# A gated linear attention with an MLP on one core: another order table for all engines, and 64 fill-in matmuls of 512 columns for 134 of 256

## The chip, the core and the metric

The kernel runs on one core of a Trainium2 chip. The core has five engines that run side by side, each in the order of its own instruction queue: PE (TensorE, matmuls), ACT (ScalarE), DVE (VectorE), POOL (GpSimd) and SP (SyncE, which here only issues DMAs). The metric is the time of one execution on the device in microseconds, as the median of several runs.

## The reference: what is computed

For each of 4 batches and 8 heads, over 768 steps, a state of 48 x 48 complex numbers decays by a gate per row and takes up the outer product of k and v; y is q times the real part of the state. Then y, with the heads put side by side (384 columns), goes through a layer norm and an MLP (384 to 1536 to 384, ReLU) and is added to its result.

```
scale = min(mag, 0.999) / (mag + 1e-6);  a = (a_re + i a_im) * scale
for t: S = a[t][:, None] * S + k[t] v[t]^T
       y[t] = q[t] . Re(S)
x = y, heads side by side;  out = x + relu(layernorm(x) * g @ w_ch1) @ w_ch2
```

## The kernel before, in words

The 768 steps of each batch are cut into 6 chunks of 128, and two chunks make a pair: 12 pairs, P = 0 to 11, and 24 chunks, n = 2P and 2P + 1. For a pair, `pair_ops` (line 393) adds named operations. The gates become a running log-decay: ln, iv, r, r2, u on ACT, DVE and POOL, then l and lc on DVE, and dec, a matmul with triangular ones on PE; e and en on ACT are the exponentials of its sum. The angles go th (arctan) on ACT, ph on PE (a running sum, taken over from pair to pair by car), sin and cos on ACT; in the first three pairs the cosine is made by a second sum, qt. The logarithms and the sines need different tables on ACT, and the operations tab.log and tab.trig load them. From this come ke = k * en, qe = q * e, and the products ks and qs with sin and cos. These are transposed to ksT and qsT, either on PE (kT, qT, then a copy out of PSUM) or by a DMA issued from SP (line 599). Then am = ksT' qsT and its masked copy atm, the state G from gm, and y and its copy x. After bn (the norm's sums), xtr and xT (the transpose of x), the MLP follows: mm1 (line 722), relu (lines 739 and 741), mm2 (line 754). The scale of the norm, rstd, is applied at the end in ot, on DVE at once or as oa on ACT and ot on POOL, and st stores it (line 777). The first weight of the MLP is corrected once by wp on PE and wc on DVE, so that the norm's mean needs no step of its own.

No program orders the work while it is built: the order is the table `PLAN` (lines 39 to 144), a list of 1160 entries such as `relu.0.0:A0`. An entry names an operation, the engine (P for PE, A for ACT, V for DVE, G for POOL, S for SP) and, where it uses PSUM, the bank. `Graph.run` (line 164) emits the operations in this order, so each engine's queue is the order of its own letters in the table. An entry with `@name` is made to wait for another operation besides its operands (line 208): such waits put POOL and DVE in turns.

A DMA is issued by the engine that the table names: SP's queue or ACT's (`ring`, line 285). Loads of k, q and vf (line 404) are one chunk of 192 KB each, are and aim (line 445) 384 KB for a pair, in halves for pair 0. Buffers go in rings (`RINGS`): three for are, aim, q and k, two for vf, five for ot. An issue on ACT's queue has its place among ACT's arithmetic. w1b and w2b, the weights, are loaded from POOL (wl).

In the table before, ACT issues aim.0.0 and aim.0.1, 18 of the 24 vf loads (from vf.3 on) and 19 of the 25 stores; SP issues the rest and the 25 transposing DMAs.

The fill-ins `warm.0` to `warm.133` (line 787) are matmuls on constants, with a result that nobody reads. They stand in PE's queue between its first real operations, up to am, y and ph of the first two pairs.

Of the kernel before, what the change touches and what calls it, by code (L numbers as in the profile page):

```python
# [59 lines left out]
warm.123:P0 car.0.1:A4 wgc:V cos.0.0:A1 qt.0.1:P4 ph.1.0:P6 k.1.1:S ks.0.1.1:V cos.0.1:A4 qs.0.1.1:V th.2.0:A  # L60
qs.0.0.1:V qs.0.1.0:V wp.1:P5 ks.0.1.0:V sin.1.0:A6 qs.0.0.0:V ks.0.0.0:V qT.1:P4 wc.1.2:V5 tab.log.2:A qT.0:P1
qsT.1:V4 kT.1:P0 qs.1.0.1:G@wc.1.2 dec.2.0:P2 car.1.0:V6 ln.3.0:A warm.124:P4 qsT.0:V1 warm.125:P4 wp.0:P4 e.2.0:A2
are.4.0:S wc.1.0:V5 kT.0:P1 en.2.0:A2 vf.1.0:S ksT.1:V0 ksT.0:A1 wc.0.0:V4 vf.1.1:S am.1:P2 warm.126:P0 wc.1.1:V5
iv.3.0:A warm.127:P0 am.0:P0 wc.0.2:V4 qt.1.0:P6 tab.trig.3:A warm.128:P5 warm.129:P5 warm.130:P5 warm.131:P5
wc.0.1:V4 warm.132:P5 warm.133:P5 atm.0:V0 ph.2.0:P4 r.3.0:G@wc.0.1 cos.1.0:A6 k.2.0:S v.0:A wp.2:P6 atm.1:V2
aim.4.0:S sin.2.0:A4 gm.0:P7 ke.1.0.0:G y.0:P0 G.0:V7 k.2.1:S x.0:A0 qt.2.0:P4 ke.1.0.1:V gm.1:P7 cos.2.0:A4 y.1:P1
q.2.0:S qs.1.0.0:V xtr.0:P0 ks.1.0.0:V x.1:A1 qT.2:P3 th.3.0:A ks.1.0.1:V qT.3:P5 qsT.2:V3 xtr.1:P1 q.2.1:S xT.0:A0
r2.3.0:G@ks.1.0.1 kT.3:P4 qsT.3:A5 xT.1:V1 kT.2:P2 ksT.3:V4 mm1.0.0.0:P0 G.1:V7 q.3.1:S tab.log.4:A v.1:G am.3:P4
ksT.2:V2 mm1.0.0.1:P0 are.5.0:S ke.2.0.0:G atm.3:V4 ln.4.0:A mm1.0.1.0:P2 q.3.0:S wl.3:G mm1.0.1.1:P2 relu.0.0:A0
wc.2.0:V6 am.2:P4 wc.2.2:V6 relu.0.1:A2 gm.2:P7 k.3.0:S atm.2:V4 ph.3.0:P0 qe.2.0.0:G@wc.2.2 G.2:A7 k.3.1:S iv.4.0:A  # L70
y.3:P2 wl.4:G wc.2.1:V6 y.2:P3 x.3:A2 gm.3:P7 pad.ks.2:G u.3.0:A mm1.0.2.0:P4 x.2:V3 r.4.0:G@wc.2.1 bn.3:V xtr.2:P6
xtr.3:P3 mm1.0.2.1:P4 xT.2:A6 xT.3:V3 G.3:V7 tab.trig.5:A mm1.1.1.0:P2 relu.0.2:V4 qe.2.0.1:G are.6.0:S mm1.1.1.1:P2
sin.3.0:A0 wl.5:G mm1.1.2.1:P6 bn.0:V vf.2.0:S relu.1.1:A2 mm1.1.0.1:P4 pad.qs.2:G l.3.0:V mm1.1.2.0:P6 abs.3.0:A0
r2.4.0:V mm1.1.0.0:P4 th.4.0:A car.3.0:V0 mm2.0.0:P2 relu.1.0:A4 ke.2.0.1:V mm2.1.0:P3 qs.2.0.1:V vf.2.1:S cos.3.0:A
lc.3.0:V mm2.2.0:P4 qs.2.0.0:V bn.2:V tab.log.6:A qT.4:P5 mm2.1.1:P3 bn.1:V rstd.1:G dec.3.0:P0 ks.2.0.1:V u.4.0:A
ks.2.0.0:V mm2.0.1:P2 rstd.0:G en.3.0:A0 l.4.0:V ksT.5:S mm2.2.1:P4 e.3.0:A0 lc.4.0:V ln.5.0:A relu.1.2:V6
qe.3.0.1:G@lc.4.0 mm2.1.2:P3 qe.3.0.0:G mm2.0.2:P2 aim.5.0:S oa.1:A3 qT.5:P0 iv.5.0:A vf.3.0:A ot.0:V2 dec.4.0:P6
qsT.4:V5 mm2.2.2:P4 e.4.0:A6 vf.3.1:A qs.3.0.1:V kT.4:P1 qs.3.0.0:V en.4.0:A6 dps.3:P5 are.7.0:S dps.4:P2 ksT.4:V1
ke.3.0.0:G@qs.3.0.0 qT.6:P3 qsT.5:A0 ph.4.0:P6 ot.2:V4 aim.6.0:S ke.3.0.1:G ln.6.0:A decc.3:V5 decc.4:V2 am.4:P4
q.4.0:S v.2:G qsT.6:V3 mm2.3.0:P1 iv.6.0:A atm.4:V4 ks.3.0.1:G k.4.0:S qT.7:P2 tab.trig.7:A mm2.3.1:P1 qsT.7:V2  # L80
gm.4:P3 am.5:P4 sin.4.0:A6 ks.3.0.0:V k.4.1:S y.4:P2 atm.5:V4 r.5.0:G@ks.3.0.0 kT.6:P0 car.4.0:A6 mm2.3.2:P1 x.4:A2
G.4:A3 ksT.6:V0 k.5.1:S kT.7:P5 abs.4.0:A6 xtr.4:P4 ot.1:G y.5:P0 ksT.7:V5 q.4.1:S th.5.0:A am.6:P6 x.5:V0 v.3:G
k.5.0:S am.7:P2 xT.4:A4 atm.6:V6 xtr.5:P0 ph.5.0:P4 r2.5.0:G xT.5:A0 cos.4.0:A ot.3:V1 gm.6:P0 mm1.2.1.1:P6 atm.7:V2
G.6:A0 vf.4.1:A r.6.0:G aim.7.0:S abs.5.0:A4 y.6:P1 mm1.2.1.0:P6 x.6:V1 sin.5.0:A4 vf.4.0:A mm1.2.2.1:P2 relu.2.1:V6
cos.5.0:A xtr.6:P1 r2.6.0:G y.7:P4 mm1.2.2.0:P2 th.6.0:A st.0:A x.7:V4 gm.7:P0 bn.7:V xtr.7:P4 tab.log.8:A ke.4.0.1:G
mm1.2.0.0:P6 xT.6:V1 mm1.2.0.1:P6 q.5.1:S xT.7:V4 qe.4.0.0:G G.7:V0 u.5.0:A are.8.0:S mm1.3.0.1:P4 bn.6:V ke.4.0.0:G
mm1.3.0.0:P4 relu.2.2:A2 st.2:A relu.2.0:V6 qe.4.0.1:G mm1.3.1.1:P0 relu.3.0:A4 ks.4.0.0:V mm1.3.2.1:P2 rstd.3:G
ks.4.0.1:V u.6.0:A mm1.3.2.0:P2 l.5.0:V ksT.8:S mm2.5.0:P6 qs.4.0.1:V ln.7.0:A mm1.3.1.0:P0 lc.5.0:V q.5.0:S
qs.4.0.0:V kT.9:P7 relu.3.1:A0 l.6.0:V dec.5.0:P4 qsT.9:S mm2.5.1:P6 iv.7.0:A lc.6.0:V ksT.9:V7 mm2.6.0:P0 en.5.0:A4
q.6.0:S r.7.0:V mm2.4.0:P1 e.5.0:A4 qT.8:P7 q.7.0:S bn.5:V v.4:A r2.7.0:G@r.7.0 dec.6.0:P4 are.9.0:S bn.4:V  # L90
relu.3.2:A2 mm2.4.1:P1 k.6.0:S qsT.8:V7 mm2.6.1:P0 rstd.2:G en.6.0:A4 qe.5.0.1:V am.8:P2 ke.5.0.0:V e.6.0:A4
mm2.4.2:P1 qe.5.0.0:V ln.8.0:A atm.8:V2 gm.8:P7 ke.5.0.1:G@qe.5.0.0 q.6.1:S am.9:P4 iv.8.0:A mm2.6.2:P0 qe.6.0.0:G
atm.9:V4 u.7.0:A st.1:A mm2.5.2:P6 ph.6.0:P2 G.8:A7 vf.6.0:A ks.5.0.1:V k.6.1:S tab.trig.9:A qs.5.0.1:V mm2.7.0:P4
ot.4:V1 abs.6.0:V2 y.8:P5 th.7.0:A vf.5.1:A mm2.7.1:P4 l.7.0:V x.8:A5 vf.5.0:A gm.9:P7 y.9:P1 sin.6.0:A2 vf.6.1:A
mm2.7.2:P4 x.9:V1 car.6.0:A2 xtr.8:P5 qs.5.0.0:V xtr.9:P1 oa.7:A4 ph.7.0:P2 xT.9:V1 qsT.10:S ks.5.0.0:G@qs.5.0.0
xT.8:V5 cos.6.0:A ot.5:V6 qT.11:P1 G.9:V7 sin.7.0:A2 mm1.4.1.0:P4 qe.6.0.1:V abs.7.0:A2 st.4:A mm1.4.1.1:P4 ksT.10:S
qs.6.0.0:V mm1.4.0.1:P6 tab.log.10:A car.7.0:V2 ke.6.0.1:G@qs.6.0.0 mm1.4.0.0:P6 qsT.11:V1 mm1.4.2.0:P2 ln.9.0:A
lc.7.0:V aim.8.0:S v.5:V mm1.4.2.1:P2 relu.4.1:A4 st.3:A relu.4.0:V6 qs.6.0.1:G@v.5 kT.11:P1 relu.4.2:A2 aim.9.0:S
# [725 lines left out]
```

## Time and profile before

| | us |
|---|---|
| median of 3 runs | 191.35 |
| lowest and highest of the runs | 191.23 and 193.47 |
| the profiled execution, its own time | 192.75 |
| its span, first to last instruction | 191.0 |
| busy in that span: PE, DVE, ACT, POOL | 177.3, 156.6, 158.9, 105.5 |
| matmuls of the fill-ins, busy | 17.5 |
| moved by DMA | 37.57 MB, 197 GB/s mean |

The profile is one execution. Busy time of PE is modelled: a matmul is listed with its passage through the array, so matmuls in a row overlap and their spacing is shorter than their duration. A wait is put down to the operation that came last before it ended. Idle time of an engine costs something only where another one waits for it in turn. L numbers are lines of the kernel.

### The profile page before, as it was taken

Reading aid. Unit: us, or ns where it says so; the run is one execution under the profiler, and the core shown is the slowest. Engines: PE = TensorE matmul, PEld = TensorE weight load, DVE = VectorE, ACT = ScalarE, POOL = GpSimd, SP = SyncE. Lnnn points to the kernel's source line nnn. Section 1 sums busy time; section 2 is a strip of 40 time slices with the busy share of each in tenths; the row PEclk is TensorE's granted clock in tenths of the full one; section 3 lists DMA queues with packets and bytes.
Section 4 is the critical chain, followed back from the end, with each engine's and each line's share of the span. In section 5 each row is a group of like instructions: output and inputs, shape, how many; then the busy total and the mean of one; then the engine's idle time right before and its main releaser. Section 6 shows DMA issues by size and latency. Waiting matters only on the chain.

```text
span 191.0 us, 5154 instructions
## 1 busy us (share of the span) xinstructions
PE 177.3 (93%) x2045; PEld 138.6 (73%) x2045; DVE 156.6 (82%) x285; ACT 158.9 (83%) x224; POOL 105.5 (55%) x124
## 2 busy tenths in 40 slices
...
GB/s 153 278 240 202 212 198 204 210 214 207 242 108 287 205 220 234 154 183 234 136 265 234 190 221 230 282 223 204 141 160 262 217 126 179 256 191 151 5 124 82
DMA packets 133080, 37.57 MB, mean 197 GB/s; under 512 B 127168, under 2 KB 133056, under 8 KB 133056
## 3 DMA queue, kind: packets, MB, share of 16 engines
...
## 4 chain that ended last, share of the span: by engine, by line
PE 63%; DVE 10%; ACT 9%; DMA 8%; issue 4%; ACTq 2%; POOL 1%; SPq 1%; DVEq 0%; POOLq 0%
PE banks L754 22%; PE banks L722 16%; PE banks L617 5%; PE banks L594 4%; DMA q<-in_q_dram 4%; DMA ksT<-ks 3%; PE banks L477 3%; PE banks L667 2%; ACTq L777 2%; PE banks L496 2%; PE banks L670 2%; DVE w1b L388 2%; DMA are<-in_a_re_dram 2%; PE banks L645 2%; PE banks L688 2%
## 5 line engine op out<-in xcount | busy, mean ns | idle before, releaser
L754 PE MATMUL banks<-w2b,h 128*128 128x384 bf16 (+1 forms) x300 | 55.7, 319 | 0.6 <-ACT h L739 0.6
L722 PE MATMUL banks<-xT,w1b 128*128 128x256 bf16 x432 | 50.9, 272 | 0.7 <-ACT h L739 0.5
L722 PEld LDWEIGHTS <-w1b 128*128 128x128 bf16 x432 | 41.4, 98 | 7.0 <-issue 1.2
L754 PEld LDWEIGHTS <-h 128*128 128x128 bf16 x300 | 26.7, 97 | 13.8 <-ACT h L739 1.0
L295 DVE TENSOR_TENSOR atm<-banks,mask 128x1024 bf16<-128x1024 f32 x24 | 29.0, 1219 | 3.8 <-PE banks L617 2.9
L739 ACT ACTIVATE h<-banks 128x1024 bf16<-128x1024 f32 (+1 forms) x26 | 25.7, 1009 | 4.6 <-DVE ks L295 2.6
L792 ACT ACT_TABLE_LOAD x19 | 24.4, 1283 | 2.6 <-PEq L808 1.3
L295 POOL TENSOR_TENSOR ke<-k,en 128x384 bf16<-128x384 f32 x17 | 15.4, 916 | 14.1 <-ACT e L481 4.3
L767 POOL TENSOR_TENSOR ot<-ot,x 128x384 f32<-128x384 f32 x13 | 12.5, 967 | 14.2 <-ACT ot L760 12.9
L295 POOL TENSOR_TENSOR r<-aim,are 128x768 f16<-128x768 f32 (+1 forms) x8 | 13.7, 1715 | 11.0 <-DVE w1b L388 4.1
L787 PE MATMUL banks<-u_e 128*128 128x256 f16 x134 | 17.5, 286 | 2.2 <-POOL u_e L323 2.2
L295 POOL TENSOR_TENSOR qs<-qe,trig 128x768 bf16<-128x768 bf16 x8 | 13.0, 1640 | 10.3 <-DVE w1b L388 7.2
L617 PE MATMUL banks<-qsT,ksT 128*128 128x128 bf16 x192 | 14.5, 219 | 2.8 <-ACT h L739 2.1
L787 PEld LDWEIGHTS <-u_e 128*128 128x128 f16 x134 | 13.5, 102 | 4.5 <-POOL u_e L323 1.9
L617 PEld LDWEIGHTS <-ksT 128*128 128x128 bf16 x192 | 12.1, 97 | 5.1 <-issue 2.8
L741 DVE TENSOR_SCALAR h<-banks 128x1024 bf16<-128x1024 f32 (+1 forms) x11 | 12.7, 1166 | 2.7 <-PE banks L722 2.7
L295 POOL TENSOR_TENSOR qe<-q,e 128x384 bf16<-128x384 f32 x12 | 11.0, 917 | 6.8 <-DVE r L295 3.6
L466 DVE SCALAR_TENSOR_TENSOR l<-r,w 128x768 f16<-128x768 f16 (+1 forms) x13 | 12.6, 969 | 1.3 <-ACT r L462 1.1
L680 DVE BATCH_NORM_STATS2 stats<-x 128x6 f32<-128x384 bf16 x24 | 13.1, 546 | 0.1
L667 PE MATMUL banks<-v,atm 128*128 128x48 bf16 x192 | 12.0, 183 | 0.0
L514 ACT ACTIVATE trig<-banks 128x768 bf16<-128x768 int16 (+1 forms) x13 | 9.8, 761 | 2.5 <-DVE car L509 2.4
L496 PE MATMUL banks<-th,u_th 128*128 128x384 f16 (+1 forms) x52 | 11.8, 313 | 0.0
...
## 6 DMA issues: line engine op xcount, KB each, us to landing
k<-in_k_dram SPq DMA_DIRECT2D x24, 192.0 KB, 5.1
q<-in_q_dram SPq DMA_DIRECT2D x24, 192.0 KB, 4.3
...
out_dram<-ot ACTq DMA_DIRECT2D x19, 192.0 KB, 3.4
vf<-in_v_dram ACTq DMA_DIRECT2D x18, 192.0 KB, 4.3
...
vf<-in_v_dram SPq DMA_DIRECT2D x6, 192.0 KB, 7.0
```

The lines of the kernel that those rows point to most:

```text
L295: {"DVE": nc.vector, "POOL": nc.gpsimd}[eng(name)].tensor_tensor(**kw)
L466: nc.vector.scalar_tensor_tensor(out=S_("l"), in0=S_("r2"), scalar=0.5, in1=S_("w"), op0=ALU.mult, op1=ALU.add)
L496: nc.tensor.matmul(heads(ps[:, c]), lhsT=u_th[:, c, j], rhs=step(T("th", P), j), start=False, stop=(j == R - 1), skip_group_check=True)
L617: nc.tensor.matmul(ps[:, h], lhsT=T("ksT", n)[:, h], rhs=T("qsT", n)[:, h], start=True, stop=True)
L667: nc.tensor.matmul(ps[:, h], lhsT=T("atm", n)[:, h], rhs=T("v", P)[:, c, h], start=True, stop=nfirst)
L680: nc.vector.bn_stats(out=T("stats", n), in_=T("x", n))
L722: nc.tensor.matmul(ps[:, jj], lhsT=w1b[:, dc, ts(gi * JG + jj, C)], rhs=T("xT", P)[:, dc].rearrange("p c t -> p (c t)"), start=(dc == 0), ...
L739: act(out=dst, in_=src, func=AF.Relu)
L741: nc.vector.tensor_scalar(out=dst, in0=src, scalar1=0.0, scalar2=None, op0=ALU.max)
L754: nc.tensor.matmul(bank(own)[:, 0:w], lhsT=T("h", P)[:, j, ts(c, C)], rhs=w2b[:, j, es], start=(j == 0), stop=(j == NJ - 1))
L787: g.add(f"warm.{i}", lambda i=i: nc.tensor.matmul(bank(f"warm.{i}")[:, 0:256], lhsT=u_e[:, 0, 0], rhs=u_e[:, 1].rearrange("p j t -> p (j t ...
L792: g.add(f"tab.{nm}.{i}", lambda tab=tab: nc.scalar.preload_act_table_set(tab))
```

## The change

The table `PLAN` is another one, with 1087 entries. All operations of the computation are kept; three oa (17, 18 and 20) fall away because their ot is made at once by DVE. The order differs on every engine, and so does the engine of 91 operations and the bank of many. Entries with `@` are 38 instead of 27. In numbers by kind:

| | before | after |
|---|---|---|
| vf loads issued by ACT, by SP | 18, 6 | 4, 20 |
| stores issued by ACT, by SP | 19, 6 | 11, 14 |
| aim.0.1 issued by | ACT | SP |
| ot on POOL, on DVE (oa on ACT) | 13, 12 (13) | 10, 15 (10) |
| r on POOL, on DVE | 8, 5 | 6, 7 |
| qs on POOL, on DVE | 8, 18 | 11, 15 |
| qe on POOL, on DVE | 12, 12 | 13, 11 |
| v on POOL, ACT, DVE | 5, 4, 3 | 7, 3, 2 |
| x on ACT, on DVE | 12, 12 | 14, 10 |
| relu on ACT to DVE, DVE to ACT | | 5, 5 |
| fill-ins | 134 | 64 |

SP's queue begins, before and after:

```
before: are.0.0 are.0.1 are.1.0 k.0.1 aim.1.0 k.0.0 are.2.0 aim.2.0 q.0.1 q.1.0 are.3.0 q.1.1 q.0.0 gln vf.0.0 aim.3.0
after:  are.0.0 are.1.0 gln are.0.1 aim.1.0 aim.0.1 are.2.0 k.0.0 k.0.1 q.0.1 q.0.0 aim.2.0 k.1.1 q.1.0 aim.3.0 q.1.1
```

ACT's queue at three places, before and after (DMA issues are vf and st):

```
before: cos.5.0 th.6.0 st.0 tab.log.8 u.5.0 relu.2.2 st.2 relu.3.0
after:  xT.5 abs.5.0 sin.5.0 G.6 cos.5.0 th.6.0 relu.2.2 tab.log.8 u.6.0 u.5.0 relu.2.0 relu.3.0
before: abs.7.0 st.4 tab.log.10 ln.9.0 relu.4.1 st.3 relu.4.2 e.7.0
after:  abs.7.0 sin.7.0 tab.log.10 ln.9.0 relu.4.1 relu.4.0 e.7.0
before: st.16 relu.10.2 st.18 st.15 st.12 rstd.10 relu.10.1 st.19
after:  oa.19 st.18 relu.10.2 G.22 relu.10.1 x.23 xT.22 oa.21 st.19
```

SP's queue where stores stand among transposes, after: `qsT.10 aim.8.0 st.5 ksT.10`, `st.4 k.7.1 qsT.12`, `st.7 q.9.0 qsT.17 st.8 ksT.16`, `ksT.18 st.9 qsT.18`, `st.14 st.11 ksT.23`.

In the start-up, car.0.0 goes from DVE to ACT, qsT.3 from ACT to DVE, r.0.1 from POOL to DVE, and qs.0.1.0, qs.0.1.1 and ks.0.1.1 from DVE to POOL. At the end relu.11.2.0 goes to ACT, with st.21 just ahead of it, and the last six stores are ACT's.

Two places of the code besides the table:

```diff
@@ f_gm
-                                         rhs=T("v", P)[:, c, h], start=nfirst, stop=True,
+                                         rhs=T("v", P)[:, c, h], start=nfirst and h == 0, stop=True,
@@ fill-ins
-    for i in range(134):
+    for i in range(64):
         g.add(f"warm.{i}", lambda i=i: nc.tensor.matmul(
-            bank(f"warm.{i}")[:, 0:256], lhsT=u_e[:, 0, 0], rhs=u_e[:, 1].rearrange(
-                "p j t -> p (j t)"), start=True, stop=True), needs=["ue"], ps=(f"warm.{i}", 1))
+            bank(f"warm.{i}"), lhsT=u_e[:, 0, 0], rhs=u_e.rearrange(
+                "p c j t -> p (c j t)"), start=True, stop=True), needs=["ue"], ps=(f"warm.{i}", 1))
```

A fill-in now writes a whole bank of 512 columns. The first, 15 of them, stand before dec.0.0, where 56 stood.

More of the change, by code (lines that the diff above doesn't have):

```diff
@@ L60 @@
[L60 to L98, printed above, removed]
-dec.7.0:P4 ksT.11:V1 k.7.1:S mm2.8.0:P6 e.7.0:A4 ke.6.0.0:V am.11:P2 en.7.0:A4 ks.6.0.0:V mm2.8.1:P6 q.7.1:S bn.9:V
@@ L140 @@
[L140 to L143 removed]
+ue:G zdec:G car0.1:G uth:V aim.0.0:A are.0.0:S tab.log.0:A ln.0.0:A iv.0.0:A r.0.0:V r2.0.0:A u.0.0:A l.0.0:V pick:G
@@ new lines @@
+qsT.4:V5 rstd.1:A qe.3.0.1:G ot.0:V2 vf.3.0:S aim.5.0:S qs.3.0.1:V oa.1:A3 ke.3.0.1:G@qs.3.0.1 dec.4.0:P6 e.4.0:A6
+aim.7.0:S kT.4:P1 v.2:G ksT.4:V1 qs.3.0.0:V mm2.2.2:P4 k.4.1:S dps.3:P5 en.4.0:A6 ln.6.0:A qT.5:P0 are.7.0:S ot.2:V4
+k.4.0:S dps.4:P2 qsT.5:A0 decc.3:V5 q.4.1:S iv.6.0:A decc.4:V2 ph.4.0:P6 qT.6:P3 ke.3.0.0:G abs.4.0:A6 ks.3.0.1:G
+qsT.6:V3 am.4:P4 atm.4:V4 qT.7:P2 qsT.7:V2 car.4.0:A6 mm2.3.0:P1 mm2.3.1:P1 tab.trig.7:A sin.4.0:A6 ks.3.0.0:V am.5:P4
+st.0:S gm.4:P3 vf.4.1:S k.5.1:S atm.5:V4 y.4:P2 x.4:A2 kT.6:P0 mm2.3.2:P1 ksT.6:V0 st.2:A kT.7:P5 ksT.7:V5 xtr.4:P4
@@ new lines @@
+ph.6.0:P2 u.7.0:A ln.8.0:A iv.8.0:A l.7.0:V vf.6.0:A tab.trig.9:A th.7.0:A mm2.5.2:P6 ot.6:V0 car.6.0:A2 abs.6.0:V2
+G.8:A7 rstd.2:G ot.4:V1 y.8:P5 qe.5.0.1:G qs.5.0.1:G qe.6.0.0:G mm2.7.0:P4 mm2.7.1:P4 y.9:P0 k.6.0:S x.9:V0 st.3:A
+mm2.7.2:P4 vf.5.1:S xtr.9:P0 x.8:A5 xtr.8:P5 gm.9:P7 ot.5:V6 sin.6.0:A2 vf.6.1:A ke.5.0.1:G vf.5.0:S ph.7.0:P2
+qs.5.0.0:G qT.11:P1 are.9.0:S lc.7.0:V xT.8:V5 qsT.10:S G.9:V7 cos.6.0:A xT.9:V0 mm1.4.0.1:P6 mm1.4.0.0:P6 oa.7:A4
+abs.7.0:A2 mm1.4.1.0:P4 qe.6.0.1:V aim.8.0:S mm1.4.1.1:P4 ks.5.0.1:V sin.7.0:A2 st.5:S tab.log.10:A ln.9.0:A
```

150 lines of the change are left out of this document (86 added, 64 removed).

## Prediction

> **What bounds the kernel now.** I read the page first, then the busy time by stage, then the waits of PE, then the chain where PE stops.
>
> ```profile
> span 191.0 us, 5154 instructions
> PE 177.3 (93%) x2045; PEld 138.6 (73%) x2045; DVE 156.6 (82%) x285; ACT 158.9 (83%) x224; POOL 105.5 (55%) x124
> ```
> ```profile
> 0.00:5.00 5.00, 2.78 (x14) 2.04 (x15) 0.85 (x1) 2.06 (x3) 3.77 (x17) 1.00 0.62 160
> 5.00:10.00 5.00, 5.00 (x47) 4.35 (x46) 3.52 (x4) 4.77 (x9) 2.14 (x7) 1.00 1.12 280
> 10.00:15.00 5.00, 5.00 (x48) 4.34 (x46) 3.79 (x7) 4.28 (x8) 1.29 (x2) 1.00 1.03 237
> ...
> 20.00:25.00 5.00, 2.08 (x15) 1.23 (x14) 3.95 (x15) 2.56 (x6) 0.00 (x0) 1.00 1.20 217
> 25.00:30.00 5.00, 4.36 (x49) 3.04 (x48) 4.94 (x11) 4.97 (x7) 1.64 (x1) 1.00 1.04 200
> 30.00:36.00 6.00, 5.56 (x79) 3.82 (x76) 6.00 (x10) 5.81 (x9) 2.69 (x2) 1.00 0.90 195
> 36.00:50.00 14.00, 13.90 (x188) 12.29 (x188) 13.55 (x25) 13.70 (x20) 10.04 (x11) 1.00 1.15 222
> 50.00:66.00 16.00, 15.97 (x195) 11.47 (x194) 15.42 (x30) 15.50 (x21) 11.00 (x12) 1.00 1.00 204
> ...
> 90.00:101.00 11.00, 8.87 (x104) 7.09 (x100) 10.38 (x21) 8.35 (x12) 4.66 (x4) 1.00 1.13 201
> ```
>
> Columns of the stages: length, then busy us and instructions of PE, PEld, DVE, ACT, POOL, then clock, DMA share, GB/s. There are two regimes. Up to 36 us the program is a start-up in which PE does mostly fill-ins and ACT and DVE make the first operands; POOL does nothing at all in 20-25. From 36 us on PE is the bound: over the whole span it is busy for 177.3 of 191.0 us, and of the stages of 14 and 16 us all but 0.13 us. Its multiplications are not changed, so a new order can win only what PE waits, and the length of the start-up. The profiled execution took 192.75 us for a span of 191.0; the median of the runs shown is 191.35, so 1.40 us less. I make the sum against the profiled span and carry the difference over to the median.
>
> ```profile
> PE banks L521 <- ACT trig L514: 2.8, 2, 2.6
> ...
> PE banks L617 <- ACT h L739: 2.1, 1, 2.1
> ...
> PE banks L754 <- ACT h L739: 0.6, 1, 0.6
> PE banks L722 <- ACT h L739: 0.5, 1, 0.5
> ...
> PE banks L722 <- ACT sh L531: 0.2, 1, 0.2
> ```
>
> Three of PE's waits after 36 us are for one thing, a relu (L739) on ACT: 2.1 + 0.6 + 0.5 = 3.2 us, and 0.2 more for ACT's abs. The 2.6 us wait for L514 lies in the start-up.
>
> **Why ACT is late at those three places.**
>
> ```profile
> 70.37 2.37 ACTq L777 DMA_DIRECT2D out_dram<-ot  x1
> ...
> 72.77 1.28 ACT L792 ACT_TABLE_LOAD   x1 [0.95 <-issue]
> ```
> ```profile
> 99.28 0.36 ACTq L777 DMA_DIRECT2D out_dram<-ot  x1
> 99.74 1.02 ACT L739 ACTIVATE h<-banks 128x1024 bf16<-128x1024 f32 x1 [2.57 <-DVE ks L295]
> ```
> ```profile
> 93.49 5.77 DMA ksT<-ks
> ```
> ```profile
> 170.83 2.45 ACTq L777 DMA_DIRECT2D out_dram<-ot  x3
> 173.33 0.20 ACT L704 ACTIVATE rstd<-mv 128x2 f32<-128x2 f32 x1 [1.53 <-DMA out_dram<-ot]
> ```
>
> Each is a store (L777) issued from ACT's own queue. At 99.28 the store stood in front of the relu and ACT was idle for 2.57 us; in the chain a transpose of ksT, issued from SP, lands 5.77 us after 93.49, at 99.26, and the store is issued right then. So the store's issue was held by a transfer of another queue. The issue itself takes 0.36 us.
>
> **The change, part by part.** (a) 23 DMA issues leave ACT for SP: 14 of the 18 vf loads, 8 of the 19 stores on balance, and aim.0.1.
>
> ```profile
> out_dram<-ot ACTq DMA_DIRECT2D x19, 192.0 KB, 3.4
> vf<-in_v_dram ACTq DMA_DIRECT2D x18, 192.0 KB, 4.3
> ```
>
> At the first place st.0 becomes SP's and st.2 stays on ACT, earlier, behind x.4. At the second, st.3 stands on ACT behind G.8, nine steps ahead of the next relu, and st.4 is SP's. At the third, of st.18, st.15 and st.12 the last two are SP's, and rstd.10 is POOL's. So I take all 3.2 + 0.2 = 3.4 us away. Bounds: at best these 3.4; at worst the late relu is replaced by another late operand and none of it remains. On SP the same issues stand among loads and transposes; behind them wait k, q, are, aim and the transposes that am needs. I cost this at nothing because loads go a pair or two ahead (three buffers of q and k, two of vf) and the vf loads that SP already issues stand there too; if that cover is gone it is the first rival.
>
> The Trainium skill (DMA: Bandwidth & Descriptors, Issuing engines are not separate DMA queues) says that issuing from several engines saves only the issuing sequencer's time, usually small beside the transfer. By that, 23 issues of 0.36 us are 8.3 us of ACT's sequencer, mostly beside its arithmetic, PE gains nothing from (a), and with the start-up the time is about 190; its chance is within that of the second rival below. The trace speaks against the word small: one issue held ACT for 2.57 us.
>
> (b) The start-up.
>
> ```profile
> 13.77 7.08 DMA q<-in_q_dram
> ...
> 22.00 0.36 DVE car L509
> ```
> ```profile
> 18.33 1.67 ACT L485 ACTIVATE th<-r 128x384 f16<-128x384 f16 x3
> 22.39 0.87 ACT L514 ACTIVATE trig<-banks 128x384 bf16<-128x384 int16 x2 [2.39 <-DVE car L509]
> ...
> 23.29 0.32 ACT L506 ACTIVATE car<-banks 32x192 f16<-32x192 int16 x1
> ```
> ```profile
> 14.40 1.04 DVE L295 TENSOR_TENSOR r<-aim,are 128x768 f16<-128x768 f32 x1 [0.96 <-ACT are L450]
> ```
>
> ACT had its angles at 20.00 and stood still for 2.39 us: the first sine waited for car on DVE, which stood behind qe, which waited for q.0.0, the 13th DMA of SP's queue. In the new table q.0.0 is the 11th, are.3.0, q.1.0 and q.1.1 come behind it, and car.0.0 is ACT's. Through aim.2.0 the new order carries 3.15 MB (eight transfers' worth of 384 KB); the stage rows moved 0.80, 1.40 and 1.19 MB in the first three 5 us, so aim.2.0 lands at about 10 + 0.95 / 0.237 = 14.0, and q.0.0 at 12.3 instead of 20.85. aim.2.0 was the 8th and is now the 12th: r.2.0, which began at 14.40, begins at 14.4 to 15.1 (the later end for what gln and the issues add, an estimate), so the angles are there at 20.0 to 20.8. The sine starts 1.6 to 2.4 us sooner; 0.32 goes to the car that ACT now makes, and I take the low end: 1.3 us. Bounds: 0 (DVE, at 4.94 of 5 and 6.00 of 6 until 36, gives nothing on) and 2.4 (the whole idle time).
>
> Does the lead reach PE? DVE passes three products (qs.0.1.0, qs.0.1.1, ks.0.1.1) to POOL and car to ACT, and takes qsT.3 from ACT, and ke.2.0.1 earlier. By the rows below this is -(3 x 0.35) - 0.36 + 0.68 + 0.65 = -0.1 us: nothing. POOL needs perhaps 0.9 us for each of the three, inside the 5 us in which it did nothing; without that cover kT.1 is late by up to 2.7 us.
>
> ```profile
> 23.03 0.35 DVE L295 TENSOR_TENSOR ks<-ke,trig 128x384 bf16<-128x384 bf16 x1
> ...
> 27.73 0.69 DVE L292 COPY qsT<-banks 128x1024 bf16<-128x1024 bf16 x1
> ```
> ```profile
> L295 POOL TENSOR_TENSOR ke<-k,en 128x384 bf16<-128x384 f32 x17 | 15.4, 916 | 14.1 <-ACT e L481 4.3 <-DVE qs L295 4.2 <-ACT en L481 4.1
> ...
> L295 DVE TENSOR_TENSOR ke<-k,en 128x384 bf16<-128x384 f32 x7 | 4.6, 656 | 0.0
> ```
>
> (c) Fill-ins.
>
> ```profile
> L787 PE MATMUL banks<-u_e 128*128 128x256 f16 x134 | 17.5, 286 | 2.2 <-POOL u_e L323 2.2
> ```
> ```profile
> 2.22 7.57 PE L787 MATMUL banks<-u_e 128*128 128x256 f16 x56 [2.22 <-POOL u_e L323]
> ...
> 16.05 2.89 PE L787 MATMUL banks<-u_e 128*128 128x256 f16 x25
> ...
> 27.85 0.81 PE L384 MATMUL banks<-w1b,gc 128*128 128x512 bf16 x3
> ```
>
> 25 in a row take (2.89 - 0.27) / 24 = 0.109 us each; the 512-column ones of L384, each 0.379 long and three in 0.81, start 0.216 apart. 64 x 0.216 = 13.8 us stand for 17.5. All lie in start-up time in which PE has nothing else, so the difference is worth nothing. A real matmul that becomes ready behind one waits up to 0.216 instead of 0.109; in twelve places half of the difference is 0.6 us, not all on the path: +0.2.
>
> (d) Engine swaps in the steady part (r, qe, qs, v, x, relu, ot among them) leave every engine's sum nearly as it was: relu moves five each way, ot gives DVE three and takes three oa from ACT. Off the path; cost 0, up to 0.7 either way in all, about one such operation. The start flag in f_gm changes no duration: 0.
>
> (e) The end: the last pair's half-relus change engines and st.21, which needs POOL's ot.21, stands on ACT ahead of relu.11.2.0. Two mm2 groups cover it. Cost 0; without the cover a bit over half a microsecond.
>
> Sum: -3.4 - 1.3 + 0.2 = -4.5 us. Profiled, 192.75 becomes 188.25; by the median, 191.35 becomes 186.85, and I say 186.8.
>
> **The rivals.** First, slower: SP as the queue in which one waits for all.
>
> ```profile
> SPq L777 <- POOL ot L767: 10.3, 3, 7.5
> ```
>
> At six places the new table has a store straight or nearly ahead of a transpose (st.5 of ksT.10, st.4 of qsT.12, st.7 of qsT.17, st.8 of ksT.16, st.9 of qsT.18, st.14 and st.11 of ksT.23). A store that is held like the one at 99.28 holds the transpose, and am on PE then loses the 2.1 us of its row. All six cost 12.6: 199.5 us. It is no gain from 4.5 us of such waits and slower by over 2% from 8.3, four places: 195.2 us, the time I give it. For it: SP waited up to 7.5 us already. Against it: none of PE's rows names a transpose, and in the new table each store stands well behind its ot.
>
> Second, no change beyond 2%: PE's waits are filled by others. In 36-66 ACT is busy 29.2 us of 30 and DVE 28.97; PE can't run ahead of them. If half of the 3.4 returns and the start-up gives nothing: 191.35 - 1.7 = 189.7. For it: those stages; against: the wait of 2.1 belongs to the relu of 99.74, and in 90-101 ACT is busy for only 8.35 of 11 us.
>
> Third, fewer fill-ins and a slow PE clock. The first 56 fill-ins took 7.57 us where 56 x 0.109 + 0.16 is 6.3: 1.3 us went to a slow start. The new table has fill-ins for 13.8 us only and PE stands still more before 36. If it falls back once for such a stretch, the work in it costs 1.3 us more, twice 2.6: 189.4. Against: PE stood still for 2.6 us at 20, and the three of 512 columns at 27.85 were 0.216 apart, the full rate. The Trainium skill (TensorE: Matmul & The Clock Gate, What's actually happening) gives about 3.4 us of idleness for the fall to half rate; the trace has no such long gap, and does not contradict it.
>
> **How the numbers follow.** Forecast 0.58 (own range 184.3 to 188.8), slower rival 0.17, no-change rival 0.19, clock 0.06. Two per cent of 191.35 is 3.8 us, about what a measurement of this kernel can tell from no change: the bounds are 187.5 and 195.2. Of the forecast's 0.58 about three quarters lie below 187.5: faster 0.44. The slower rival is over 195.2 in 0.13; the rest, 0.43, is within. The range takes the low end from all start-up idle time (191.35 - 3.4 - 2.4 = 185.5, less 0.7 twice for the swaps and the small waits: 184.1) and the high end from the slower rival with three of its places (191.35 - 4.5 + 6.3 = 193.1).
>
> **What would show it.** PE's waits for h L739 under 1 us in all, no store issue over 1 us ahead of an ACT instruction, ACT's first L514 near 21 us: right. A PE row naming DMA ksT or qsT, or SP waits for ot in mid-kernel: the first rival. Fill-ins over 0.4 us apart after 10 us: the third. The forecast is wrong if PE's waits after 36 us sum to more than 2 us for any cause, or if PE's dense part does not begin over half a microsecond sooner.

## The result and the profile after

The changed kernel takes 193.50 us (median of 16 executions, 192.42 to 196.1), the kernel before, run beside it, 191.09 us (16 executions, 189.35 to 193.47). The ratio is 1.0146, with a 95% interval of 1.0118 to 1.0175. So the change costs 1.5%, some 2.8 us by the ratio. The forecast was 186.8, with a range up to 193.1. The ratios leave out executions over 1.5% above the fastest of the same kernel; the medians are of all executions.

The page of the changed kernel, its span and its busy time:

```profile
span 192.1 us, 5012 instructions
PE 179.5 (93%) x1973; PEld 131.8 (69%) x1975; DVE 156.0 (81%) x281; ACT 157.9 (82%) x223; POOL 105.7 (55%) x126
```

The profiled execution took 193.95 us, close to its median. PE is busy for about as long as before. What changed is where it waits. The stages of the changed kernel, with the columns of the prediction's table of stages:

```profile
20.00:25.00 5.00, 4.50 (x27) 2.25 (x27) 3.62 (x11) 4.50 (x10) 2.60 (x6) 1.00 1.22 214
25.00:30.00 5.00, 3.10 (x36) 2.18 (x37) 4.84 (x9) 2.87 (x4) 3.21 (x3) 1.00 0.91 181
30.00:36.00 6.00, 5.22 (x51) 3.13 (x52) 5.86 (x8) 5.39 (x7) 4.02 (x4) 1.00 1.04 237
36.00:50.00 14.00, 13.16 (x199) 11.07 (x195) 11.67 (x20) 12.60 (x19) 9.16 (x10) 1.00 1.07 188
...
90.00:101.00 11.00, 10.63 (x125) 8.24 (x124) 10.67 (x22) 10.05 (x14) 7.13 (x6) 1.00 0.86 196
```

90 to 101 us, where PE lost 2.1 us before, is nearly full now: 10.63 of 11. But 36 to 50 us, full before (13.90 of 14), has 0.84 us of idle time, and in 25 to 30 ACT, which was busy for 4.97 of 5 us before, is busy for 2.87. PE's waits behind 40 us in the changed kernel (all rows of the view), and its longest wait between 5 and 40 us:

```profile
PE banks L715 <- DVE xT L285: 0.5, 1, 0.5
PE banks L660 <- DVE atm L288: 0.3, 1, 0.3
PE banks L681 <- DVE x L285: 0.3, 1, 0.3
PE banks L660 <- DVE car L502: 0.3, 1, 0.3
PE banks L610 <- DMA qsT<-qs: 0.2, 1, 0.2
PE banks L470 <- DVE l L462: 0.2, 1, 0.2
```
```profile
PE banks L780 <- ACT en L474: 1.6, 1, 1.6
```

(Lines of the changed kernel are 7 lower: its L732 is the relu of L739.) No row names a relu any more. Five of the six rows name DVE, one a transpose. The 1.6 us is a fill-in that waits for a bank until en.2.0 has read it. What stood ahead of en.2.0 on ACT, and what DVE waited for a little sooner:

```profile
25.76 0.81 ACT L474 ACTIVATE e<-banks 128x768 bf16<-128x768 f32 x1
28.69 0.84 ACT L441 ACTIVATE w<-are 128x768 f32<-128x768 f32 x1 [2.12 <-DMA are<-in_a_re_dram]
29.44 0.79 ACT L474 ACTIVATE en<-banks 128x768 bf16<-128x768 f32 x1
30.13 0.83 ACT L443 ACTIVATE are<-w 128x768 f32<-128x768 f32 x1
30.86 1.00 ACT L283 COPY ksT<-banks 128x1024 bf16<-128x1024 bf16 x1
```
```profile
18.94 0.47 DVE L462 TENSOR_SCALAR l<-l 128x768 f16<-128x768 f16 x1
21.38 0.80 DVE L288 TENSOR_TENSOR qe<-q,e 128x384 bf16<-128x384 f32 x1 [1.97 <-DMA q<-in_q_dram]
```

These are two of the three loads that the new order moved behind q.0.0: are.3.0 for ln.3.0 (L441) and q.1.1 for qe.1.0.1. Each wait holds all that stands behind it on its engine: en.2.0 and ksT.0 on ACT, the products of pair 0 on DVE. The first MLP matmul, mm1.0.0.0, starts at 39.57; before, it was 38.10.

### The profile page after: what moved, and what is told of

It is laid out like the page before. It is cut to its first block, busy times and chain, and to the rows that moved or that the text cites. A ratio compares the mean times of both kernels' runs of the same rounds, so it can differ in the third digit from the quotient of the medians.

```text
span 192.1 us, 5012 instructions
## 1 busy us (share of the span) xinstructions
PE 179.5 (93%) x1973; PEld 131.8 (69%) x1975; DVE 156.0 (81%) x281; ACT 157.9 (82%) x223; POOL 105.7 (55%) x126
## 4 chain that ended last, share of the span: by engine, by line
PE 47%; DMA 13%; ACT 12%; DVE 10%; SPq 6%; POOL 5%; issue 5%; DVEq 0%; ACTq 0%; POOLq 0%
PE banks L747 15%; PE banks L715 14%; DMA are<-in_a_re_dram 6%; PE banks L610 3%; PE banks L587 3%; DMA qsT<-qs 2%; SPq L397 2%; DMA k<-in_k_dram 2%; DMA aim<-in_a_im_dram 2%; SPq L438 2%; PE banks L660 2%; PE banks L489 2%; ACT h L732 2%; PE banks L470 2%; POOL ks L288 2%
## 5 line engine op out<-in xcount | busy, mean ns | idle before, releaser
L747 PE MATMUL banks<-w2b,h 128*128 128x384 bf16 (+1 forms) x300 | 53.8, 319 | 0.0
L732 ACT ACTIVATE h<-banks 128x1024 bf16<-128x1024 f32 (+1 forms) x26 | 25.6, 1008 | 6.6 <-PE banks L715 6.6
L288 POOL TENSOR_TENSOR ke<-k,en 128x384 bf16<-128x384 f32 x17 | 16.9, 1001 | 16.1 <-ACT en L474 7.8
L780 PE MATMUL banks<-u_e 128*128 128x512 f16 x64 | 18.5, 430 | 3.8 <-POOL u_e L316 2.2
L288 POOL TENSOR_TENSOR qs<-qe,trig 128x768 bf16<-128x768 bf16 (+1 forms) x11 | 16.5, 1507 | 2.4 <-ACT trig L507 1.6
L288 POOL TENSOR_TENSOR r<-aim,are 128x768 f16<-128x768 f32 x6 | 10.9, 1814 | 10.6 <-DVE ks L288 4.4
L288 POOL TENSOR_TENSOR qe<-q,e 128x384 bf16<-128x384 f32 x13 | 12.6, 970 | 5.9 <-ACT e L474 2.2
L780 PEld LDWEIGHTS <-u_e 128*128 128x128 f16 x64 | 6.5, 108 | 11.1 <-issue 5.6
L459 DVE SCALAR_TENSOR_TENSOR l<-r,w 128x768 f16<-128x768 f16 (+1 forms) x13 | 12.1, 930 | 1.5 <-ACT r L455 1.4
L441 ACT ACTIVATE w<-are 128x768 f32<-128x768 f32 (+1 forms) x13 | 10.2, 792 | 3.6 <-DMA are<-in_a_re_dram 3.5
L660 PEld LDWEIGHTS <-atm 128*128 128x128 bf16 x192 | 10.6, 96 | 2.6 <-DVE atm L288 1.2
```

Of the source, the lines that this page charges most:

```text
L288: {"DVE": nc.vector, "POOL": nc.gpsimd}[eng(name)].tensor_tensor(**kw)
L459: nc.vector.scalar_tensor_tensor(out=S_("l"), in0=S_("r2"), scalar=0.5, in1=S_("w"), op0=ALU.mult, op1=ALU.add)
L660: nc.tensor.matmul(ps[:, h], lhsT=T("atm", n)[:, h], rhs=T("v", P)[:, c, h], start=True, stop=nfirst)
L732: act(out=dst, in_=src, func=AF.Relu)
L747: nc.tensor.matmul(bank(own)[:, 0:w], lhsT=T("h", P)[:, j, ts(c, C)], rhs=w2b[:, j, es], start=(j == 0), stop=(j == NJ - 1))
L780: g.add(f"warm.{i}", lambda i=i: nc.tensor.matmul(bank(f"warm.{i}"), lhsT=u_e[:, 0, 0], rhs=u_e.rearrange("p c j t -> p (c j t)"), start=T ...
```

## The experiments

Theory 1: the loss lies in the start-up, in the loads that were moved behind. Rival: it lies in the order behind the start-up (SP's queue, engine swaps, other neighbours on PE). Runs named a_ edit the changed kernel, b_ the kernel before, and h_ joins the two orders. The ratio is always to the kernel before, run on the same chip in turn with it. "mm1" is where the profile's first matmul of mm1.0.0.0 starts, "rest" the time from there to the start of PE's last matmul, both of the one profiled execution, whose time stands beside them. That time differs from the median by up to 3.8 us (b_issue_sp), so the ratios decide.

| run | ratio | 95% interval | median us | mm1 | rest | profiled |
|---|---|---|---|---|---|---|
| before | 1 | | 191.09 | 38.10 | 148.86 | 192.75 |
| after | 1.0146 | 1.0118-1.0175 | 193.50 | 39.57 | 149.11 | 193.95 |
| a_are3_early | 1.0225 | 1.0151-1.0298 | 198.07 | 44.98 | 149.57 | 199.84 |
| b_are3_late | 0.9992 | 0.9962-1.0021 | 190.80 | 36.42 | 147.46 | 189.62 |
| b_issue_sp | 0.9974 | 0.9929-1.0019 | 191.25 | 40.30 | 148.93 | 195.05 |
| a_issue_act | 1.0433 | 1.0376-1.0490 | 199.63 | 39.91 | 154.58 | 199.98 |
| h_bstart | 1.0100 | 1.0067-1.0133 | 192.50 | 36.31 | 149.27 | 191.01 |
| h_astart | 1.0040 | 1.0006-1.0074 | 191.99 | 38.89 | 146.99 | 191.97 |
| a_are3_swap | 1.0116 | 1.0087-1.0146 | 193.12 | 37.87 | 148.84 | 191.98 |
| a_ln3_later | 1.0116 | 1.0078-1.0154 | 193.19 | 38.77 | 150.18 | 194.22 |
| b_st_behind | 0.9955 | 0.9925-0.9986 | 190.01 | 36.16 | 148.26 | 190.40 |
| h_cut50 | 1.0041 | 1.0012-1.0069 | 191.51 | 37.16 | 149.03 | 191.62 |
| h_cut94 | 1.0046 | 1.0009-1.0083 | 191.39 | 36.70 | 149.12 | 191.32 |
| h_cut135 | 1.0015 | 0.9985-1.0045 | 190.96 | 36.27 | 149.05 | 190.52 |
| a_mid_b | 1.0160 | 1.0115-1.0204 | 193.73 | 38.93 | 149.31 | 193.50 |
| a_no_warm62 | 1.0139 | 1.0094-1.0185 | 193.43 | 39.16 | 149.43 | 193.87 |
| a_x2_dve | 1.0157 | 1.0109-1.0206 | 193.48 | 39.18 | 148.99 | 193.43 |
| b_both | 0.9964 | 0.9929-0.9998 | 190.10 | 36.37 | 146.90 | 189.14 |
| a_prod_dve | 1.0233 | 1.0177-1.0288 | 195.21 | 40.63 | 150.50 | 196.32 |
| a_swap_prod | 1.0193 | 1.0143-1.0242 | 194.14 | 38.66 | 149.94 | 193.79 |

**The late load, moved to the front or put late in the kernel before.** a_are3_early and b_are3_late, SP's queue:

```diff
-after:  aim.2.0 k.1.1 q.1.0 aim.3.0 q.1.1 vf.0.0 are.3.0
+after:  aim.2.0 are.3.0 k.1.1 q.1.0 aim.3.0 q.1.1 vf.0.0
-before: q.1.0 are.3.0 q.1.1 q.0.0 gln vf.0.0
+before: q.1.0 q.1.1 q.0.0 gln vf.0.0 are.3.0
```

> The new table with one entry moved: are.3.0 is issued right behind aim.2.0 instead of behind vf.0.0, four DMAs earlier. In the new table's profile ACT stands still for 2.12 us before ln.3.0, with en.2.0 and ksT.0 behind it, because are.3.0 lands at 28.7 us (16.8 in the table before). Theory 1 (the late are.3.0 made the start-up longer): the wait before ln.3.0 is gone, the first mm1 starts 1 to 2 us sooner than at 39.57, and the time falls from 193.5 to about 192. Theory 2 (the loss is in the steady part, SP's full queue): the wait goes but the time stays at 193.5 within 0.4.

> The table before with one entry moved: are.3.0 behind vf.0.0, as in the new table, all else as before. Theory 1: ACT waits about 1 to 1.5 us before ln.3.0, with e.2.0 and en.2.0 behind it, and the time rises from 191.1 to about 192.3. Theory 2: no difference beyond 0.4 us.

In the first, ACT's wait went, but 384 KB more now stood ahead of q.1.1, and it came 6 us later than in the changed kernel. DVE, PE and the stage table of a_are3_early:

```profile
27.55 0.56 DVE L286 TENSOR_TENSOR qe<-q,e 128x384 bf16<-128x384 f32 x1 [7.99 <-DMA q<-in_q_dram]
```
```profile
28.36 1.46 PE L375 MATMUL banks<-w1b,gc 128*128 128x512 bf16 x3 [4.97 <-DVE gc L366]
```
```profile
25.00:30.00 5.00, 1.64 (x4) 0.65 (x5) 2.45 (x9) 3.86 (x5) 0.00 (x0) 0.66 0.78 150
30.00:36.00 6.00, 6.00 (x45) 3.85 (x43) 4.92 (x10) 0.61 (x1) 3.87 (x4) 0.72 1.12 257
```

DVE stood 7.99 us, PE 4.97 us, and PE's granted clock (the third column from the end) was 0.66 and 0.72 in these two rows. The ratio is 1.0225. It is a miss for both theories, with the lesson that a load moved forward delays another. In the second, are.3.0 landed at 22.5 and no one waited for it: before's order bears the later load. The time is the same.

**The same load against one of its own size.** a_are3_swap, SP's queue, and a_ln3_later, ACT's:

```diff
-q.1.0 aim.3.0 q.1.1 vf.0.0 are.3.0
+q.1.0 are.3.0 q.1.1 vf.0.0 aim.3.0
```
```diff
-e.2.0 ln.3.0 en.2.0 iv.3.0 ksT.0 tab.trig.3
+e.2.0 en.2.0 ksT.0 ln.3.0 iv.3.0 tab.trig.3
```

> The changed kernel with are.3.0 and aim.3.0, two loads of the same size, exchanged in SP's queue, so that no other load moves. Theory 1, the late are.3.0 holds ACT's ln.3.0 and with it am.1 and mm1: are.3.0 lands near 18.3 instead of 28.66, aim.3.0 near 28.7, ACT's wait of 2.1 us at 26.6 goes, mm1.0.0.0 starts 1 to 1.5 us sooner than 39.57, and the time is 192.0 to 192.5. Rival, the products on POOL and late q.1.1 hold the start-up anyway: mm1.0.0.0 within 0.4 us of 39.57, time 193.5.

> The changed kernel with ln.3.0 and iv.3.0 on ACT moved behind ksT.0, no load moved: what stood behind the waiting ln.3.0 (en.2.0, ksT.0) no longer waits for the load. Theory 1: am.1 starts 1 to 1.5 us sooner than 31.14, PE's wait of 1.6 us of a fill-in for en goes, mm1.0.0.0 1 us sooner, time 192.5. Rival, POOL and q.1.1 hold the start-up: 193.5 or, as ln.3.0 with its followers is later, 194.

With the exchange ACT no longer waits:

```profile
25.64 0.81 ACT L472 ACTIVATE e<-banks 128x768 bf16<-128x768 f32 x1
26.35 0.83 ACT L439 ACTIVATE w<-are 128x768 f32<-128x768 f32 x1
27.09 0.80 ACT L472 ACTIVATE en<-banks 128x768 bf16<-128x768 f32 x1
```

ln.3.0 starts 2.34 us sooner, mm1 1.7 us, and the ratio falls only from 1.0146 to 1.0116. The other edit gives the same 1.0116. The two point the same way, 0.3% or 0.6 us each, but the intervals overlap that of the changed kernel. So the load is probably a part of the loss, and a small one; neither run alone shows it.

**Half and half.** The two tables hold almost the same operations up to mm1.0.0.0, so one can be continued by the other. h_bstart is before's order to there and then the changed one, h_astart the reverse.

```diff
 h_bstart: PLAN = before[.. mm1.0.0.0] + (after, without what is done)
 h_astart: PLAN = after[.. mm1.0.0.0] + (before, without what is done)
```

> Before's order up to the first matmul of the MLP (mm1.0.0.0) with its 256-column fill-ins, then the order of the changed kernel. Theory 1, the loss lies in the start-up: from mm1.0.0.0 on, the changed kernel's profile took 147.9 us to mm2.23.2.1, before's 148.6, so this runs as before in the start-up and 0.7 us less after it: 190.4 us, ratio 0.996. Rival, the loss lies in the order behind the start-up (SP's queue, the swaps): 193 to 193.5 us, ratio over 1.01.

> The changed order with its 512-column fill-ins up to mm1.0.0.0, then before's order. Theory 1, the loss lies in the start-up: 1.5 us late at mm1.0.0.0 as in the changed kernel's profile, and up to 1.5 more by the first mm2: 192.6 to 194 us, ratio 1.008 to 1.015. Rival, the loss lies behind the start-up: about 191, ratio 1.00.

1.0040 and 1.0100 add up to nearly the 1.0146 of the whole, which speaks against a large cost of the two seams by themselves. The start-up costs 0.4%, some 0.8 us; the order behind it 1.0%, 1.9 us. Theory 1 explains the smaller part, the rival the larger. The profiles say so too: with the changed order behind the start, the rest is 148.84 to 150.50 us, mean 149.5 in nine profiles (the changed kernel's among them; a_issue_act and those with mixed stretches left out), with before's own order 148.86, 147.46 and 146.99 (before, b_are3_late, h_astart), mean 147.8. And the changed order brings most of its waits after either start. All rows of h_bstart behind 45 us:

```profile
PE banks L720 <- DVE xT L290: 0.5, 1, 0.5
PE banks L665 <- DVE atm L293: 0.3, 1, 0.3
PE banks L686 <- DVE x L290: 0.3, 1, 0.3
PE banks L665 <- DVE car L507: 0.3, 1, 0.3
PE banks L720 <- ACT sh L529: 0.2, 1, 0.2
PE banks L475 <- DVE l L467: 0.2, 1, 0.2
```

Five of the six are rows of the changed kernel too. The waits can also be counted from the starts of PE's matmuls, from mm1.0.0.0 on: start to start, less the usual spacing of a matmul of that width. In the nine profiles of the changed order there are 10 to 12 pauses of over 0.2 us each, 3.6 to 5.6 us in all (the changed kernel: 11, 3.9 us). In the three of before's order there are 3, 4 and 6, with 2.8 to 4.0 us (the kernel before: 4, 4.0 us).

**Later cuts.** The same as h_bstart, with before's order up to the first mm2, to mm1.4.0.0 and to mm1.7.0.0.

```diff
-before[.. mm1.0.0.0] + after
+before[.. mm2.0.0] + after          h_cut50
+before[.. mm1.4.0.0] + after        h_cut94
+before[.. mm1.7.0.0] + after        h_cut135
```

> Before's order up to the first mm2 (about 50 us), then the changed order. The hybrid cut at mm1.0.0.0 (36 us) had 1.0100. Theory: the changed order loses in many places of 0.3 to 0.7 us; by the profiles 1 to 1.5 of its waits lie between the two cuts (y.3 and the mm1 behind xT), so 191.3 us, ratio 1.003 to 1.005. Rival, the loss lies in one late place (the transposes behind stores in SP's queue): still 1.01.

> Before's order up to mm1.4.0.0 (about 94 us), then the changed order. Theory of many small places: 1.002 to 1.004, the waits for transposes at xtr.9, y.11 and y.12 (1.3 us in the changed kernel's profile) still in it. Rival, one late place: still 1.01.

> Before's order up to mm1.7.0.0 (about 135 us), then the changed order. Theory of many small places: 0.998 to 1.002, as the changed order's waits behind 135 us (1 us) are about those of before (1.1). Rival, the loss lies at the end, in the stores and the last pairs: still 1.005 to 1.01.

From 1.0100 to 1.0041, 1.0046 and 1.0015: the largest step, 0.6%, between the cuts at 36 and at 50 us (their intervals just touch), nothing seen to 94, perhaps 0.3% to 135. The first rival of the prediction, stores ahead of transposes in SP's queue, lies behind 50 us in all its six places; there is no step of its size there.

**Is it the stretch from 36 to 50 us?** Three kernels change it in the changed one: a_mid_b has before's order there, a_no_warm62 lacks the two fill-ins in it, a_x2_dve has x.2 on DVE again.

```diff
 a_mid_b: after[.. mm1.0.0.0] + before[.. mm2.0.0] + after
 a_no_warm62: PE  -warm.62 -warm.63 (between gm.2 and y.3)
 a_x2_dve: ACT -x.2 (behind x.3);  DVE +x.2 (ahead of bn.2), G.3 behind xT.3
```

> The changed order, but with before's order for the stretch from mm1.0.0.0 to the first mm2 (36 to 50 us in the profile of before, 39.6 to 52.5 in the changed one). If that stretch costs 0.6% by itself, as the step between the cuts at 36 and at 50 us says: 1.0146 - 0.0059 = 1.009, 192.4 us. Rival, the step was one of before's start running into the changed stretch: still 1.0135 or more.

> The changed kernel without its two fill-ins behind mm1.0.0.0 (warm.62 and warm.63, 0.43 us of PE between gm.2 and y.3). If they hold PE's work: 193.1 us, ratio 1.0123, y.3 0.4 us sooner against mm1.0.0.0. Rival, y.3 waits for its operand in any case (0.27 us of wait stand behind the two fill-ins in the profile): ratio 1.0146, the wait before y.3 0.7 us, as in the hybrid cut at 36 us, which has no fill-ins there.

> The changed kernel with the copy x.2 on DVE again, as before, instead of behind x.3 on ACT, and G.3 behind xT.3 on DVE. If the engine swap of x makes xT.3 late for mm1.1.1.1 (PE's wait of 0.62 us at 48 us): that wait goes, mm2.0.0 starts 0.6 us sooner against mm1.0.0.0 than 12.95, ratio 1.011. Rival, the wait goes and comes back at the next place: 1.0146.

1.0160, 1.0139 and 1.0157: none can be told from the changed kernel. PE's first waits behind the seam, in h_cut50 and then in a_mid_b, suggest why:

```profile
PE banks L475 <- DVE l L467: 1.3, 1, 1.3
```
```profile
PE banks L468 <- DVE l L460: 0.8, 1, 0.8
```

PE waited at dec.3.0 in both, for lc.3.0, which on DVE stands behind both products qs.2.0.1 and qs.2.0.0. The changed kernel has no wait there: lc.3.0 is done at 52.52 and dec.3.0 starts at 53.83; its row of 0.2 for l is a wait at 81 us. So in a_mid_b time won in the stretch is lost at DVE's next operand. (A seam adds to it: what before's order does later piles up there on DVE.) The step between the cuts isn't explained by this: h_cut50 has the longer wait and is the faster one. Without the two fill-ins PE stands still for 0.70 us ahead of y.3 instead of 0.27, by the spacing of its matmuls: the 0.43 us of fill-ins were covered. In a_x2_dve PE's pause ahead of mm1.1.1.1 stayed at 0.62 us by the same spacing: x.2's engine is not its cause. The rows of the changed kernel around it:

```profile
47.80 0.33 PE L681 MATMUL banks<-ident,x 128*128 128x128 bf16 x3
48.58 4.10 PE L715 MATMUL banks<-xT,w1b 128*128 128x256 bf16 x36 [0.45 <-DVE xT L285]
```
```profile
48.17 0.36 DVE L285 COPY xT<-banks 128x384 bf16<-128x384 bf16 x1
```

PE transposes x.3 at 47.80, DVE copies the result at 48.17, PE needs it at once. In before's order mm1.0.2.1, 0.65 us of matmuls, stands between the two; in the changed one it comes ahead of xtr.3. In a_mid_b, which has before's order here, this pause is gone, and the 0.8 us at dec.3.0 stands in its place.

**The issues by themselves.** b_issue_sp is the kernel before with 28 DMA issues on SP that the change puts there, nothing moved. a_issue_act is the changed kernel with the same 28 on ACT. b_st_behind is the kernel before with six stores still on ACT, each behind the relu that it stood ahead of.

```diff
 b_issue_sp, a_issue_act: 14 vf (vf.3.0 to vf.11.1) and 14 st (st.0 to st.16): A -> S, S -> A
 b_st_behind, ACT's queue:
-th.6.0 st.0 tab.log.8 u.5.0 relu.2.2 st.2 relu.3.0
+th.6.0 tab.log.8 u.5.0 relu.2.2 st.0 relu.3.0 st.2
-relu.4.1 st.3 relu.4.2
+relu.4.1 relu.4.2 st.3
-relu.10.2 st.18 st.15 st.12 rstd.10 relu.10.1
+relu.10.2 rstd.10 relu.10.1 st.18 st.15 st.12
```

> The table before with the issuing queue of 14 vf loads and 14 stores changed from ACT to SP, no entry moved; this is part (a) of the prediction alone. The prediction's theory: PE's waits for the relu on ACT (3.2 us in the profile) go, and the time falls from 191.1 to about 188. Rival (SP as the queue in which one waits for all): loads and transposes come late and the time is 192 or more. If the 2.1 us wait at 98 us of the profile of before was of that one execution only, the gain is about 1 us at most.

> The new table with the same 28 loads and stores issued by ACT again, no entry moved. The prediction's theory: ACT is held in front of relus again and the time rises from 193.5 by 1 to 3 us. Rival (SP crowded): the loads come sooner and the time falls by 1 us or more. No difference within 0.4: the issuing queue is not what moved the time.

> The kernel before with six stores on ACT, those that stood straight ahead of the relus that PE waited for, moved straight behind them (st.3 behind relu.4.2, st.0 behind relu.2.2, st.2 behind relu.3.0, st.18, st.15 and st.12 behind relu.10.1); nothing else. If the 3.2 us of relu waits were worth their size, as the sum had it: 188 to 188.8 us, ratio 0.985 to 0.99. Rival, PE's lead over ACT and DVE is what sets the pace, and a wait that is taken away comes back within some 20 us as others: the waits for h go from the profile, others of 0.3 to 1 us take their place, 190.2 to 191, ratio 0.995 to 1.0.

b_st_behind is faster, by 0.45% (0.14 to 0.75): 0.9 us of the 3.4 that the sum had, nearer to what the rival expected. The relu waits went, and PE's longest wait became this (PE, then ACT):

```profile
90.33 0.32 PE L490 MATMUL banks<-car,pick 128*128 128x384 f16 x1 [1.50 <-ACT car L504]
```
```profile
89.35 0.40 ACTq L402 DMA_DIRECT2D vf<-in_v_dram  x1
89.80 0.48 ACT L504 ACTIVATE car<-banks 32x384 f16<-32x384 int16 x1 [1.72 <-DMA k<-in_k_dram]
```

A vf load, issued from ACT and held until a k load had landed, stood ahead of car. It is the same kind of wait as the store's at 99.28, some 8 us sooner counted from mm1.0.0.0. Nor does before's order always have the store's wait: h_astart, which has that order and those stores behind the changed start, issues the same store in 0.36 us, and the vf load 8 us ahead of it takes 1.68 us (ACT):

```profile
90.19 1.68 ACTq L395 DMA_DIRECT2D vf<-in_v_dram  x1
...
98.16 0.36 ACTq L768 DMA_DIRECT2D out_dram<-ot  x1
98.62 1.02 ACT L730 ACTIVATE h<-banks 128x1024 bf16<-128x1024 f32 x1 [0.40 <-PE banks L585]
```

In b_issue_sp, with those issues on SP, PE waits for a transpose that SP issues:

```profile
155.03 0.62 PE L615 MATMUL banks<-qsT,ksT 128*128 128x128 bf16 x8 [1.11 <-DMA ksT<-ks]
```

and no difference in time is seen. In the changed order the same move is worth 2.8% (1.0433 against 1.0146): with the issues back on ACT its waits for h return, 1.2 and 1.0 us, and PE waits 1.0 us for a transpose and 0.9 us for ACT's x besides. The worth of an issue's engine belongs to an order, not to the issue.

**The two small edits of before together.** b_both is b_st_behind with are.3.0 late.

```diff
 b_st_behind, SP's queue:
-q.1.0 are.3.0 q.1.1 q.0.0 gln vf.0.0
+q.1.0 q.1.1 q.0.0 gln vf.0.0 are.3.0
```

> The kernel before with the six stores moved behind their relus (0.9955 by itself) and are.3.0 moved behind vf.0.0 in SP's queue (0.9992 by itself). If the two add up: 0.9947, 189.9 us. Rival, the earlier start lets PE's lead over ACT and DVE run out all the same: 0.9955 to 1.000.

0.9964, about as b_st_behind alone, as the rival had it. b_st_behind (190.01 us, beside 190.88) and b_both (190.10, beside 190.90) are faster than the kernel before, by about 0.4%.

**The three products on POOL.** a_prod_dve and a_swap_prod, which has the exchange of are.3.0 as well:

```diff
-POOL: qs.0.1.0 qs.0.1.1 ks.0.1.1
-DVE: ks.0.1.0 ks.0.0.0 qs.0.0.0 wc.1.2
+DVE: ks.0.1.0 qs.0.1.1 ks.0.0.0 qs.0.0.0 qs.0.1.0 ks.0.1.1 wc.1.2
```

> The changed kernel with qs.0.1.0, qs.0.1.1 and ks.0.1.1 on DVE again. If POOL's ks.0.1.1 (25.70 to 26.61) is what makes kT.1 and with it am.1 late: kT.1 0.5 to 1 us sooner than 27.62, but ln.3.0 still holds ksT.0 until 28.69, so am.1 and mm1.0.0.0 at most 0.3 us sooner: 193.2 to 193.5 us, ratio 1.013 to 1.0146. Rival, the products hold the start-up by themselves: 192.5, ratio 1.009.

> The changed kernel with are.3.0 and aim.3.0 exchanged and the three products on DVE again. If late load and products are together what the start-up loses: am.1 near 28, mm1.0.0.0 near 36.5, and what remains is what the hybrid with before's start had: ratio 1.010, 192.5 us. Rival, PE's lead over ACT and DVE is used up behind the start-up in any case, or something else holds the start-up: as the exchange alone, 1.0116, 193.1 us.

Both are slower than without the edit, by 0.8 to 0.9%: against 1.0146, and 1.0193 against 1.0116. Neither theory had it. DVE, in the changed kernel busy for 4.84 of 5 and 5.86 of 6 us from 25 to 36 us, has no room there; three products of 0.35 us more on it cost 1.5 to 1.7 us.

## Why the prediction was wrong, step by step

**(a), the relu waits, -3.4.** The mechanism was right: the changed kernel has no such wait. The size was wrong, and with it "I cost this at nothing". Taken away alone, the waits were worth 0.9 us (0.3 to 1.4): PE waited at other places instead, longest 1.50 us for ACT's car. Taken away by issuing from SP, no gain can be told (0.9974, up to 1.0019): in the one profile PE waited 1.1 us for a transpose and 0.8 and 0.7 us for DVE instead. And the 2.1 us was not a fixed part of before's order, as h_astart shows. The bound "none of it remains" was the nearer end. The text itself had the fact that should have decided: "In 36-66 ACT is busy 29.2 us of 30 and DVE 28.97; PE can't run ahead of them." The rule of the Trainium skill (DMA: Bandwidth & Descriptors, Issuing engines are not separate DMA queues) came nearer for the kernel before: b_issue_sp agrees with it, though single issues did hold ACT. In the changed order, where a_issue_act is 2.8% slower, the runs don't agree with it.

**(b), the start-up, -1.3.** Two errors. The first is the base. The 2.39 us that ACT stood still was not a property of the order. Of seven profiles with before's own load order, two have it (before, and b_issue_sp with 2.35); in five, q.0.0 landed at 17.7 to 17.9 instead of 20.8 and ACT waited 0 to 0.58 us there. ACT in b_st_behind:

```profile
18.26 1.67 ACT L483 ACTIVATE th<-r 128x384 f16<-128x384 f16 x3
20.45 0.87 ACT L512 ACTIVATE trig<-banks 128x384 bf16<-128x384 int16 x2 [0.52 <-DVE car L507]
```

In these five mm1 starts at 36.2 to 37.2, not at 38.10. The profiled execution was 1.40 us over the median, and I "carry the difference over" as if it lay nowhere; by these profiles it most likely lay in this very wait. The second error is what was left out. q.0.0 came as foreseen, at 13.5 (12.3 said), aim.2.0 at 14.8 (14.0 said), r.2.0 at 14.84 and the first sine at 20.27. But "are.3.0, q.1.0 and q.1.1 come behind it" was never priced. They cost ACT 2.12 and DVE 1.97 us; against the 36.2 to 37.2 of the usual start mm1 is 2.4 to 3.4 us late. By the hybrids, 0.8 us of that is left at the end. The three products on POOL were costed rightly at nothing; on DVE they would cost more.

**(c), fill-ins, +0.2.** Right in sense: the fill-ins behind mm1.0.0.0 cover a wait and cost nothing that can be measured.

**(d), swaps and order, 0 up to 0.7.** This step failed most. The order behind the start costs 1.9 us (1.0%, 0.67 to 1.33). I compared engines by their sums; by the rows what counts is how much PE has between an operand's source and its use. The profiles show the loss as many waits, most of 0.2 to 0.6 us: 10 to 12 pauses of PE in place of 3 to 6. In seven of the nine profiles the two fill-ins behind mm1.0.0.0 lie in that time too, but without them nothing was won. The cuts put most of it ahead of 50 us, but before's order in that stretch alone gives nothing back. Which single edits make it stays open.

**(e), the end, 0.** Not tried alone; the changed order from 135 us on is at 1.0015 (0.9985 to 1.0045).

**The rivals.** The first, slower, had the sign but not the cause: the changed kernel's one row for a transpose is 0.2 us. The second, no change, described the mechanism best (waits filled by others) and stopped at no gain. The third did not happen in the changed kernel, whose clock is 1.00 in every stage shown, but the clock fell in the profiles of two experiments. Of the signs that would make the forecast wrong, the dense part did not begin sooner (39.57), and PE's waits behind 36 us passed 2 us: 1.8 in the rows behind 40 us, 0.26 ahead of mm1.0.0.0 at 39.57, and those too small for the view.
